# Three of seven second-layer products by a second level of Strassen, in a fused retention and MLP kernel

## The chip, the cores and the metric

The kernel runs on one core of a Trainium2 chip. A core has a matrix engine (TensorE, "PE" in the profile, with its weight loads as "PEld"), a vector engine (VectorE, "DVE"), a scalar engine (ScalarE, "ACT"), GpSimd ("POOL") and a sync engine ("SP") that here issues nearly all transfers; 16 DMA engines carry them. Matrix products are written to PSUM, eight banks of 128 rows by 512 f32; everything else lives in SBUF. The metric is device time in microseconds: 638.29 us, the median of three runs (638.23 to 638.30).

## The reference, cut to what matters

```python
# attention: B=4 heads H=8, S=768 tokens, D=64
state = gamma[None, :, None, None] * state + np.einsum('bhd,bhe->bhde', k[:, :, t], v[:, :, t])
y[:, :, t] = scale * np.einsum('bhd,bhde->bhe', q[:, :, t], state)
# x = y as (B*S, H*D) = (3072, 512); then two layers, 512 -> 2048 -> 512
h = x @ w_in
g = np.maximum(0.01 * h, h)
return (g @ w_out).astype(np.float32)
```

All is float32. The change lies in the last line, the second layer.

## The kernel before, in words

**Tiling.** The sequence is cut into six chunks of 128 tokens (`c` = 0 to 5; with the four batches 512 rows each), the hidden width of 2048 into four units of 512 (`u` = 0 to 3). For each chunk the attention gives `x`, and each unit adds a first layer, a leaky ReLU and a second layer to the chunk's output `o`.

**Strassen (Winograd's form).** Both layers are products of 2 x 2 blocks, made with seven products instead of eight. M1 to M7 take weight blocks (four given, three sums: indices 0 to 6 of a unit) and moving blocks: `g[0..3]`, and the sums `gd[0..2]` that `differences` makes (L609; four subtractions: gd0 = g1 - g0, gd1 = g3 - gd0, gd2 = g2 - gd1, then g1 becomes g3 - g1). In `seven` (matmuls at L662) one product of the second layer is four matmuls of 128 x 128 weights with 256 columns: 28 for a visit. Each float32 matmul shows in the profile as two instructions.

**Chunks 2 to 5, first layer.** There the first layer goes down a second level: each of its seven products is again seven, on blocks of 128. A visit has 49 such matmuls of 128 columns (L1184), in two groups: inner group 0 (four outer products, weights `wa`) and inner group 1 (three, weights `wb`), in the order M1, M5, M4, M6, M2, M3, M7 of `INNER`. ScalarE copies M1's result into M6's bank (L1188) and takes M5, M4, M6 and M2 out of PSUM (L1190 to L1196); VectorE adds M3 and M7 (L606). `outer` then sums these into `g` (two sums after group 0, six after group 1) and ScalarE applies the leaky ReLU (L1226). The weights, sums included, were written to DRAM (`kept`) and are loaded anew for each visit by `load_unit` (L1061 to L1066): 1792 KB for `wa` when inner group 0 has read the old ones, 1344 KB for `wb` after inner group 1.

**The loop around the change.** A visit `n` = 0 to 15 is (chunk 2 + n // 4, unit n % 4). The order is written out by hand: each engine does its work in program order, each instruction when what it needs is there. Visit n does: `differences` of g of n; inner group 0 of visit n+1; the attention of the next chunk in units 0 and 1 (`joint_visit`, L427 and L444, which ends with a load of v and two `decay_v` on GpSimd, L161); then the second layer of n in the order `FUSED`: M1, M5, M6, (scores of the attention to come, L369 and L380, masked by L387), M2, inner group 1 of n+1, M7, `outer` of n+1, M3, M4. In PSUM M1 and M2 share bank A, M6 and M7 B, M5 and M3 C, M4 has D; A to D are banks 5, 4, 7, 6, the inner products use 0 to 3. M1 is copied to B (L755) so that M6 and M7 add onto it, and M7's sum to D (L776) for M4. The output `o` has four blocks of 512 columns; in unit 0 they are set by ScalarE (L746), else VectorE adds (L606), and in unit 3 each is stored (L742). The last visit, 15, has no first layer beside it and uses the order `LAST`: M1, M5, M6, M4, M2, M7, M3.

**Words used below.** "The leaves" are the second-level products of the change; "the tail" is what lies behind visit 14.

Of the kernel before, what the change touches and what calls it, by code (L numbers as in the profile page):

```python
# [9 lines left out]
FP32 = mybir.dt.float32  # L10
# [6 lines left out]
ALU = mybir.AluOpType  # L17

C = 128
# [3 lines left out]
def kernel(  # L23
# [14 lines left out]
    nc = tc.nc  # L38
    NC = S // C
    DM = H * D  # L40
    HP = H // 2
    NU = DF // 512
    N = B * C // 2
# [20 lines left out]
    units = {}  # L64
# [15 lines left out]
    def unit(k):  # L80
        if k not in units:
            units[k] = unit_tile(k, f"w{k}")
        return units[k]

    def block(k, i):

        if k < N_UNITS - 1:
            return unit(k)[:, i]
        return units[k][i // 2][:, i % 2] if i < 6 else last_s4[:, 0]

    gq = dec[:, 0 : HP * C].rearrange("p (j m t) -> p j m t", j=2, t=C)
# [236 lines left out]
    room = {}  # L328
# [169 lines left out]
    def following(c, b):  # L498

        at = (c, b + 2) if b == 0 else (c + 1, 0)  # L500
        return at if at[0] < NC else None
# [5 lines left out]
    TOP = 1151  # L507
    BEND = 2048 + 896 - TOP

    def piece(n):  # L510

        k, h, i = n // 4, n // 2 % 2, n % 2
        if k < N_UNITS - 1:
            return unit(k)[:, 2 * h : 2 * h + 2, i, :]
        new_pair(h)
        return units[k][h][:, :, i, :]
# [88 lines left out]
    def plus(out, a, b):  # L605
        nc.vector.tensor_tensor(out=out, in0=a, in1=b, op=ALU.add)  # L606

    def minus(out, a, b):
        nc.vector.tensor_tensor(out=out, in0=a, in1=b, op=ALU.subtract)  # L609
# [189 lines left out]
        return [x, new_t(c, f"t_{c}")]  # L799

    slot = [0]

    def new_g(c, u):
        i = slot[0]
        slot[0] = 1 - i
        g = work.tile([128, 4, 2, N], FP32, tag=f"g{i}", name=f"g_{c}_{u}")
        gd = work.tile([128, 3, 2, N], FP32, tag=f"gd{i}", name=f"gd_{c}_{u}")
        return u, g, gd

    def run(steps, at):  # L810

# [233 lines left out]
    def sums(c, group):  # L1045
        return lambda: sums_of_x(c, group)

    streamed = []
    N2 = (NC - 2) * NU

    def at_of(n):
        return 2 + n // NU, n % NU
# [15 lines left out]
    def begin_units():  # L1068

        streamed.append(work.tile([128, 7, 4, C], FP32, tag="late4", name="wa"))  # L1070
        load_unit(0, 0)
        flat = work.tile([128, 28 * C], FP32, tag="late6", name="wb")
        streamed.append(flat[:, 0 : 21 * C].rearrange("p (j i n) -> p j i n", j=7, i=3))

    def next_heads():
        for b in range(2):
# [83 lines left out]
    def part_of(moving, s):  # L1160

        block, sums = moving
        if s in (2, 3, 4):
            return sums[:, s - 2]
        k, t = divmod((0, 2, None, None, None, 3, 1)[s], 2)
        return block[:, k, ts(t, C)]

    INNER = (("M1", 0, 0, 0), ("M5", 1, 3, 2), ("M4", 2, 2, 4), ("M6", 3, 4, 3), ("M2", 0, 1, 1),
             ("M3", 1, 5, 5), ("M7", 3, 6, 6))
# [72 lines left out]
    def products(steps, n):  # L1242

        for _ in range(n):
            next(steps, None)
# [35 lines left out]
    for n in range(N2):  # L1281
# [18 lines left out]
            xs[c + 1] = new_x(c + 1)  # L1300
        if visiting:
            joint_visit(c + 1, 2 * u)
        steps = output(c, os[c], [gs.pop(n)], u == 0, u == NU - 1, room=room if more else last_room,
                       order=FUSED if more else LAST, held=held if more else None)
        products(steps, 3)
        if c + 1 < NC and u < 2 and following(c + 1, 2 * u):
            scores_of_pair(*following(c + 1, 2 * u))
        if visiting:
            load_unit(n + 2, 0)
        products(steps, 1)  # L1310
        if c + 1 < NC and u == 1:
            differences(*xs[c + 1])
        if c + 1 < NC and u == 2:
            sums_of_x(c + 1, 0)
        if more:
            inner(n + 1, 1)
            for i in range(2) if visiting else ():
                ahead(c + 2, 2 * u + i)
            products(steps, 1)
            outer(n + 1, 1)  # L1320
        if n + 2 == N2:
            differences(*gs[n + 1][1:])
        products(steps, 3)
# [92 lines left out]
```

## Time and profile before

| what | value |
|---|---|
| median of three runs | 638.29 us |
| the profiled execution | 637.82 us |
| its span, first to last instruction | 636.0 us |
| PE / PEld / DVE / ACT / POOL busy | 99 / 89 / 73 / 42 / 4% |
| chunks 2 to 5 begin at about | 240 us |
| DMA, mean over the span | 178 GB/s |
| HBM read / written | 93.35 / 19.14 MB |
| queue q1 (the transfers that SP issues) | 53.2% of 16 engines |

How to read it: the profile is of one execution, and times in it are microseconds from its first instruction. A group of instructions is told by line, engine, operation, output tile <- input tiles, shape and count; behind the bar stand the busy time in all, the mean nanoseconds of one, and the idle time of the engine just before, with what ended most of it. A timeline line has start, duration and the merged instructions. A matmul's recorded duration overlaps the next one's; the distance of starts is what it costs. For DMAs the number behind the size is the median time from issue to landing. No DMA of the kernel before is issued by GpSimd.

### The profile page before, as it was taken

To read this page: it belongs to the slowest core of one execution; us is meant where nothing else is said; L and a number is where in the kernel's file an instruction comes from. 1 tells how busy PE (TensorE), PEld (TensorE's weight loads), DVE (VectorE), ACT (ScalarE), POOL (GpSimd) and SP (SyncE) were. 2 spreads that over 40 slices of the span, in tenths; PEclk is the share of its full clock that TensorE was granted. 3 is DMA by queue.
4 is the path that set the end of the run, shared out by engine and by line. 5 is a ranking of instruction groups with operands and counts; after the bars stand their busy time and mean duration, and the time that the engine had idled before them with its cause. 6 is when DMAs were issued, how large, how long until landed. Compare 5 with 4: busy or idle time off the path is not lost.

```text
span 636.0 us, 14285 instructions
## 1 busy us (share of the span) xinstructions
PE 628.8 (99%) x6086; PEld 568.8 (89%) x6086; DVE 464.1 (73%) x760; ACT 268.9 (42%) x515; POOL 23.3 (4%) x45
## 2 busy tenths in 40 slices
PE   8999999999999999999999999999999999999997
PEld 5888888888888889899999999999999999999996
DVE  5679769889979986576785666877737768636655
ACT  4876556347343124242352442423433423534421
POOL 2000000000011010101000101000010000000000
PEclk9999999999999999999999999999999999999999
DMA  8941426556863998376735392864455236444201
GB/s 331 404 131 38 128 67 220 148 174 194 283 250 110 351 333 280 103 238 193 259 88 184 120 295 79 268 195 140 137 169 185 87 123 197 154 162 158 87 1 68
DMA packets 87537, 113.42 MB, mean 178 GB/s; under 512 B 3241, under 2 KB 71721, under 8 KB 87473
## 3 DMA queue, kind: packets, MB, share of 16 engines
q1 hardware_dynamic: 87168, 111.88, 53.2%
q8 instruction: 48, 0.79, 0.5%
q10 hardware_dynamic: 304, 0.62, 0.3%
q14 instruction: 17, 0.13, 0.1%
HBM read 93.35 MB, written 19.14 MB: 177 GB/s over the span
## 4 chain that ended last, share of the span: by engine, by line
PE 95%; DVE 2%; ACT 1%; DMA 1%; issue 0%; DVEq 0%; ACTq 0%
PE bank L662 32%; PE bank L1184 27%; PE C_h L662 4%; PE B_o L662 4%; PE A_h L662 4%; PE C_o L662 4%; PE A_o L662 4%; PE B_h L662 4%; PE D_h L662 2%; PE D_o L662 2%; PE d L683 2%; PE bank L369 1%; PE bank L444 1%; PE bank L427 1%; PE bank L380 1%; DMA t<-decay_dram 1%
## 5 line engine op out<-in xcount | busy, mean ns | idle before, releaser
L606 DVE TENSOR_TENSOR made<-made,bank 128x512 f32<-128x512 f32 (+1 forms) x96 | 56.4, 618 | 55.9 <-PE bank L1184 51.5
L606 DVE TENSOR_TENSOR o<-o,bank 128x512 f32<-128x512 f32 (+2 forms) x91 | 58.5, 661 | 51.8 <-PE bank L662 31.2
L662 PE MATMUL bank<-g,w 128*128 128x256 f32 x384 | 89.9, 382 | 0.0
L662 PEld LDWEIGHTS bank<-g,w 128*128 128x128 f32 x384 | 70.7, 190 | 9.2
L1184 PEld LDWEIGHTS bank<-x,wb 128*128 128x128 f32 x672 | 77.6, 192 | 0.8
L1184 PE MATMUL bank<-x,wb 128*128 128x128 f32 x672 | 77.6, 275 | 0.0
L1184 PE MATMUL bank<-x,wa 128*128 128x128 f32 x512 | 67.7, 275 | 0.0
L662 PE MATMUL bank<-gd,w 128*128 128x256 f32 x288 | 66.1, 379 | 0.0
L1184 PEld LDWEIGHTS bank<-x,wa 128*128 128x128 f32 x512 | 63.5, 192 | 1.1 <-ACT made L1194 0.2
L662 PEld LDWEIGHTS bank<-gd,w 128*128 128x128 f32 x288 | 54.7, 190 | 7.4
L1184 PE MATMUL bank<-t,wa 128*128 128x128 f32 x384 | 53.3, 275 | 0.0
L1226 ACT ACTIVATE g<-g 128x512 f32<-128x512 f32 x64 | 39.3, 631 | 30.8 <-DVE g L606 30.8
L1184 PEld LDWEIGHTS bank<-t,wa 128*128 128x128 f32 x384 | 48.0, 192 | 0.0
L1188 ACT COPY bank<-bank 128x512 f32<-128x512 f32 (+1 forms) x32 | 16.7, 520 | 67.8 <-PE bank L1184 67.5
L606 DVE TENSOR_TENSOR g<-made 128x512 f32<-128x512 f32 x64 | 42.7, 688 | 1.2
L755 ACT COPY bank<-bank 128x512 f32<-128x512 f32 x17 | 9.7, 570 | 71.2 <-PE bank L662 71.1
L609 DVE TENSOR_TENSOR gd<-g,gd 128x512 f32<-128x512 f32 x48 | 33.2, 692 | 5.4 <-ACT g L1226 0.5
L776 ACT COPY bank<-bank 128x512 f32<-128x512 f32 x16 | 9.1, 570 | 46.4 <-PE bank L662 46.4
L662 PE MATMUL bank<-g,last 128*128 128x256 f32 x120 | 28.3, 380 | 0.0
L662 PE MATMUL bank<-gd,last 128*128 128x256 f32 (+1 forms) x124 | 27.5, 373 | 0.0
L662 PE MATMUL A_h<-x,w 128*128 128x256 f32 x112 | 26.6, 380 | 0.0
L662 PEld LDWEIGHTS bank<-gd,last 128*128 128x128 f32 x124 | 22.8, 190 | 3.2 <-DVE gd L609 0.3
(223 smaller groups left out, 1030.1 us busy)
## 6 DMA issues: line engine op xcount, KB each, us to landing
wa<-kept SPq DMA_DIRECT2D x16, 1344.0 KB, 7.2
raw<-in_weights_dram SPq DMA_DIRECT2D x31, 512.0 KB, 4.4
wb<-kept SPq DMA_DIRECT2D x16, 896.0 KB, 5.7
wa<-kept SPq DMA_DIRECT2D x16, 448.0 KB, 4.4
wb<-kept SPq DMA_DIRECT2D x16, 448.0 KB, 6.3
out_dram<-o SPq DMA_DIRECT2D x23, 256.0 KB, 3.1
kept<-w SPq DMA_DIRECT2D x12, 448.0 KB, 6.0
qk<-in_qk_dram SPq DMA_DIRECT2D x10, 512.0 KB, 8.0
```

Source lines behind the costliest of these rows:

```text
L369: nc.tensor.matmul(at[j][ts(h, 64), n, m, i], lhsT=x[ts(j, 64), 1, a, ts(h, 64)], rhs=x[ts(j, 64), 0, a, ts(h, 64)], start=(n == 0 and a = ...
L380: nc.tensor.matmul(sums[h][ts(j, 64), n, a], lhsT=key[ts(h, 64), 2 * a + j], rhs=val[ts(h, 64), 2 * a + j], start=(n == 0 and a == 0), sto ...
L427: mm = nc.tensor.matmul(at[n][j][ts(i, 64), m, ts(h, 64)], lhsT=by_half[h][ts(j, 64), n, a], rhs=x[ts(j, 64), 0, a, ts(h, 64)], start=(n = ...
L606: nc.vector.tensor_tensor(out=out, in0=a, in1=b, op=ALU.add)
L609: nc.vector.tensor_tensor(out=out, in0=a, in1=b, op=ALU.subtract)
L662: nc.tensor.matmul(to, lhsT=block(w, sa)[:, k, ts(i, 128)], rhs=rhs[:, k, a:z], start=(first and (i == 0 or split) and n == 0 and k == 0), ...
L683: nc.tensor.matmul(banks[r][:, i, :], lhsT=block(2 * u, r + 2 * kh)[:, k, ts(i, 128)], rhs=x[:, 2 * kh + th, k, :], start=(step == 0 and i ...
L755: nc.scalar.copy(out=bank_of("B"), in_=ps)
L776: nc.scalar.copy(out=bank_of("D"), in_=ps)
L1184: nc.tensor.matmul(ps[q][:, i], lhsT=w[:, j, i], rhs=part_of(moving[i], s), start=(i == 0 and m in ("M1", "M5", "M4")), stop=True, skip_gr ...
L1188: nc.scalar.copy(out=ps[3], in_=ps[0])
L1226: nc.scalar.activation(g[:, i], g[:, i], AF.Prelu, alpha=0.01)
```

## The change

In visits 4 to 14 (chunks 3, 4 and 5, without the very last unit) the second layer no longer runs by `output`. It has two parts:

- `trunk`: M1, M5, M6, M7 as before, 16 matmuls of 256 columns, on banks A, C, B, B. M7's result goes to o2 and o3 in one VectorE addition of 1024 columns (M7 is no longer copied to D); `trunk_taken` adds A to o0, and C to o1 and o3 in one.
- the leaves: M2, M4 and M3 are each cut into seven products of 128-blocks, 21 matmuls of 128 columns. `leaf_sums` makes the moving sums by four subtractions of 384 columns on GpSimd; `load_rows` loads the weights, 1344 KB a visit in three transfers on SP's queue; `leaf_steps` runs the products on banks 6, 7, 2, 5, behind M7, with the leaky ReLUs of the next visit put between its steps; `leaf_results_taken` adds the result to o0..o2, by a DMA of 768 KB issued by GpSimd that accumulates into `o`, or, in unit 3, by three VectorE additions followed by the stores.

In chunk 2 `sums_of_rows` makes the leaves' weight sums on VectorE, and `keep` writes them to DRAM (1344 KB a visit). The blocks 3, 4, 6 of the odd units change places so that those of M2, M3, M4 lie side by side, `g` and `gd` share one tile with `gd` reversed for the same reason, and two pieces of the next chunk's work (`differences(*xs[c + 1])` in unit 1, `sums_of_x` in unit 2) are issued ahead of M1, M5, M6 instead of behind M2. The scratch for DMA descriptors of GpSimd goes from 256 to 512.

```diff
+    PLACE = {3: 4, 6: 3, 4: 6}
     def block(k, i):
         if k < N_UNITS - 1:
-            return unit(k)[:, i]
+            return unit(k)[:, PLACE.get(i, i) if k % 2 else i]
...
     def new_g(c, u):
-        g = work.tile([128, 4, 2, N], FP32, tag=f"g{i}", name=f"g_{c}_{u}")
-        gd = work.tile([128, 3, 2, N], FP32, tag=f"gd{i}", name=f"gd_{c}_{u}")
-        return u, g, gd
+        both = work.tile([128, 7, 2, N], FP32, tag=f"g{i}", name=f"g_{c}_{u}")
+        last_three[c, u] = both[:, 2:5]
+        return u, both[:, 0:4], Reversed(both)
...
+    def sums_of_rows(u):
...
+            plus(r[0], a21, a22)
+            minus(r[1], r[0], a11)
+            minus(r[2], a12, r[1])
+            minus(r[3], a11, a21)
...
+        def keep():
+            for which, blocks in bases:
+                nc.sync.dma_start(out=leaf_kept[u][:, which, 0], in_=blocks[:, :, 0, 0:C])
+                nc.sync.dma_start(
+                    out=leaf_kept[u][:, which, 1:3].rearrange("p i j n -> p i (j n)"),
+                    in_=blocks[:, :, 1])
+            for j, r in enumerate(more):
+                nc.sync.dma_start(out=leaf_kept[u][:, :, 3 + j], in_=r)
...
+    def load_rows(n):
...
+        for to, kept_rows in zip(leaf_weights, (leaf_kept[at_of(n)[1]][:, i] for i in range(3))):
+            nc.sync.dma_start(out=to, in_=kept_rows)
...
+    def by_leaves(n):
+        return n >= NU and n < N2 - 1
+
+    def leaf_sums(n):
...
+        b11, b12, b21, b22 = (three[:, :, k, ts(h, C)] for k in range(2) for h in range(2))
+        for out, a, b in ((made[0], b12, b11), (made[1], b22, made[0]), (made[2], b21, made[1]),
+                          (b12, b22, b12)):
+            nc.gpsimd.tensor_tensor(out=out, in0=a, in1=b, op=ALU.subtract)
+        return [b11, b21, *made, b22, b12]
+
+    def leaf_steps(n, moving):
+        ps = [bank[i][:, 0 : 3 * C].rearrange("p (i n) -> p i n", i=3) for i in (6, 7, 2, 5)]
+        results = leaf_results()
+        for m, q, j, s in INNER:
+            for i in range(3):
+                nc.tensor.matmul(ps[q][:, i], lhsT=leaf_weights[i][:, j], rhs=moving[s][:, i],
+                                 start=(i == 0 and m in ("M1", "M5", "M4")), stop=True,
+                                 skip_group_check=True)
+            if m == "M1":
+                nc.scalar.copy(out=ps[3], in_=ps[0])
+            elif m == "M3":
+                plus(results[:, :, 1], results[:, :, 1], ps[1])
+            elif m == "M7":
+                plus(results[:, :, 3], results[:, :, 3], ps[3])
+                plus(results[:, :, 2], results[:, :, 2], ps[3])
+            else:
+                nc.scalar.copy(out=results[:, :, {"M5": 3, "M4": 2, "M6": 1, "M2": 0}[m]],
+                               in_=ps[q])
+            yield
...
+    def leaf_results_taken(c, o, final):
+        results = leaf_results()
+        if not final:
+            nc.gpsimd.dma_start(out=o[:, 0:3].rearrange("p i k n -> p (i k n)"),
+                                in_=results.rearrange("p i q n -> p (i q n)"), accum_op=ALU.add)
+            return
+        for i in range(3):
+            plus(o[:, i], o[:, i], results[:, i].rearrange("p (k h) n -> p k (h n)", k=2))
+            nc.sync.dma_start(out=out[c, i], in_=o[:, i])
...
+    def trunk_taken(o, first):
+        if first:
+            nc.scalar.copy(out=o[:, 0], in_=room["A"])
+            nc.scalar.copy(out=o[:, 3], in_=room["C"])
+            plus(o[:, 1], o[:, 1], room["C"])
+        else:
+            plus(o[:, 0], o[:, 0], room["A"])
+            plus(o[:, 1:4:2], o[:, 1:4:2],
+                 room["C"].unsqueeze(1).to_broadcast([128, 2, 2, N]))
...
         if visiting:
             joint_visit(c + 1, 2 * u)
+            if by_leaves(n):
+                load_rows(n)
...
+        moving = leaf_sums(n) if by_leaves(n) else None
...
+        if by_leaves(n):
+            steps = trunk(c, os[c], part, u == 0, u == NU - 1)
...
+        if by_leaves(n):
+            if scores_next and u > 0:
+                products(steps, 2)
+            trunk_taken(os[c], u == 0)
+            if scores_next and u == 0:
+                products(steps, 2)
+        else:
+            products(steps, 1)
+        if c == 2:
+            keep = sums_of_rows(u)
         if more:
             inner(n + 1, 1)
...
+            if c == 2:
+                keep()
             products(steps, 1)
-            outer(n + 1, 1)
+            later = [] if by_leaves(n) else None
+            outer(n + 1, 1, later)
+        if by_leaves(n):
+            products(steps, 1)
+            leaves = leaf_steps(n, moving)
+            for count, ready in ((4, 3), (1, 1)) if scores_next else ((1, 1), (3, 2), (1, 1)):
+                products(leaves, count)
+                for _ in range(ready):
+                    later.pop(0)()
+            products(leaves, 8)
+            leaf_results_taken(c, os[c], u == NU - 1)
+        if more and by_leaves(n + 1) and not (at_of(n + 1)[0] + 1 < NC and at_of(n + 1)[1] < 2):
+            load_rows(n + 1)
```

## The prediction

> **What bounds the kernel now.** I read the page's busy shares and its chain first, then windows over chunks 2 to 5, then the timeline of one visit. The page:
>
> ```profile
> PE 628.8 (99%) x6086; PEld 568.8 (89%) x6086; DVE 464.1 (73%) x760; ACT 268.9 (42%) x515; POOL 23.3 (4%) x45
> ...
> PE 95%; DVE 2%; ACT 1%; DMA 1%; issue 0%; DVEq 0%; ACTq 0%
> ```
>
> TensorE is the bound and 95% of the chain. Windows over the changed stages (length, busy PE, PEld, DVE, ACT, POOL, clock, DMA share, GB/s):
>
> ```profile
> 345.00:455.00 110.00, 110.00 (x1155) 102.42 (x1154) 77.27 (x131) 42.50 (x80) 4.48 (x8) 1.00 0.57 182
> 455.00:560.00 105.00, 105.00 (x1014) 98.13 (x1013) 72.90 (x123) 39.26 (x72) 2.43 (x6) 1.00 0.47 147
> 560.00:619.00 59.00, 59.00 (x390) 55.13 (x389) 31.94 (x52) 23.08 (x43) 0.00 (x0) 1.00 0.32 101
> ```
>
> TensorE has no gap here at clock 1.00: time falls only if it is issued less work, and rises by each stall. VectorE is at 70%, DMA at about half. A busy PE overstates one matmul (ends are modelled), so I price by pitch, start to start, in visit 6's timeline:
>
> ```profile
> 405.88 0.38 PE L1184 MATMUL bank<-x,wa 128*128 128x128 f32 x2
> ...
> 412.13 1.89 PE L662 MATMUL bank<-g,w 128*128 128x256 f32 x8
> ...
> 419.04 4.85 PE L1184 MATMUL bank<-x,wb 128*128 128x128 f32 x42
> ...
> 423.73 1.46 PE L662 MATMUL bank<-g,w 128*128 128x256 f32 x6
> ```
>
> One f32 matmul is two instructions. From 412.13 to 419.04 stand four products of 8: 6.91/32 = 0.2159 us each, 1.727 us a product. From 419.04 to 423.73 stand three second-level products: 4.69/42 = 0.1117 us. Inner group 0 takes 412.13 - 405.88 = 6.25 us.
>
> **TensorE's share of the change.** A product by seven leaves costs 14 x 0.1117 = 1.563 us, 0.164 less. Three products in each of visits 4 to 14 are 33: **-5.40 us**. The pattern (three matmuls to a weight, one bank, 128 columns) is that of inner group 1, so I take its pitch. Nothing else leaves TensorE; 632.9 is the floor.
>
> **One visit after**, from t = 0 at the end of inner group 1: M7 to 1.73, leaves to 6.42, next inner group 0 to 12.67, M1, M5, M6 to 17.85, inner group 1 to 22.54 (visits with attention are longer, with M7 ahead of t = 0). Durations:
>
> ```profile
> L606 DVE TENSOR_TENSOR o<-o,bank 128x512 f32<-128x512 f32 x81 | 54.5, 685 | 50.9 <-PE bank L662 31.2 <-ACT bank L776 19.7
> L1226 ACT ACTIVATE g<-g 128x512 f32<-128x512 f32 x64 | 39.3, 631 | 30.8 <-DVE g L606 30.8
> ...
> L606 DVE TENSOR_TENSOR made<-made,bank 128x384 f32<-128x384 f32 x48 | 25.2, 552 | 44.8 <-PE bank L1184 44.0
> ...
> L1190 ACT COPY made<-bank 128x384 f32<-128x384 f32 x16 | 7.7, 478 | 3.3 <-PE bank L1184 3.3
> ```
>
> In a run of VectorE operations the 512-wide start 0.61 us apart (617.76, 618.37, 618.97 in the last visit), so queues are counted with 0.61.
>
> *VectorE.* Out go six sums of o, 6 x 0.685 = 4.11. In come 0.685 twice and two 1024-wide ones, not in the trace: 685 + 4 x (685 - 552) = 1.22 each, 3.81 together; three leaf sums 3 x 0.552 = 1.66; in visits 7 and 11 three final sums, 2.06. So +1.4 a visit, +3.4 in those two. The queue runs: inner sums to 1.3, six outer sums to 5.0, M7's to 6.1, leaf M3 to 6.7, leaf M7 to 7.6 (its matmuls end at 6.42), differences to 10.1. M5 wants the first difference at 14.4, 6 us after it is made: hidden. If VectorE fell 6 us behind, all of it would count.
>
> *ScalarE.* It interleaves five leaf copies with four leakies. M1's copy is done by 3.1, the first leaky by 3.7, M5, M4, M6 by 5.1; leaf M7 wants M6's bank free at 5.75. Slack 0.65 us; past it each us of lateness in each visit is TensorE's. I take 0. In visit 12 (first, no attention) three 512-wide copies (o1, o0, o3) now stand between M6 and inner group 1's first copy, 0.51 apart: that copy ends 2.2 us after M6, and inner M6 wants it at 3 x 0.67 = 2.0: **+0.3**.
>
> *GpSimd* gets four 384-wide subtractions a visit. Its row is decay's 512-wide 1.04 us, so 0.8 each, 3.2 together. They start after the third difference (9.5) and are wanted at 24.3. In visits 4, 5 and 8 they queue behind the decays, which wait for a v load (4.5 us); 3.6 us of slack stays.
>
> ```profile
> 203.93 2.60 POOL L161 TENSOR_TENSOR v<-v,dec 128x512 f32<-128x512 f32 x2 [1.56 <-DMA v<-in_kv_dram]
> 204.22 1.42 DVE L609 TENSOR_TENSOR last<-last,last 128x512 f32<-128x512 f32 x1
> ...
> 363.06 2.04 POOL L161 TENSOR_TENSOR v<-v,dec 128x512 f32<-128x512 f32 x2 [4.54 <-DMA v<-in_kv_dram]
> ```
>
> Side by side, a VectorE operation on two SBUF inputs goes from 0.69 to 1.42 and GpSimd's pair from 2.04 to 2.60. The Trainium skill (SBUF — State Buffer, "Who interferes with whom") speaks against the change: with two SBUF inputs VectorE's second comes over the interface that GpSimd reads by, and in its rule of thumb the later one blocks fully. By the rule VectorE waits out up to 3.2 us a visit; by the row it loses half of the overlap, some 1.6, worst in visits 7 and 11, where sums for the next chunk lie there. Either fits in the 6 us: 0 taken.
>
> *The accumulating DMA*, 768 KB, issued by POOL at about 7.7. The trace has none. Near rows (KB each, us to landing):
>
> ```profile
> wa<-kept SPq DMA_DIRECT2D x16, 1344.0 KB, 7.2
> ...
> wb<-kept SPq DMA_DIRECT2D x16, 896.0 KB, 5.7
> wa<-kept SPq DMA_DIRECT2D x16, 448.0 KB, 4.4
> ...
> out_dram<-o SPq DMA_DIRECT2D x23, 256.0 KB, 3.1
> ```
>
> A plain one is between 448 and 896: 5.3 us. Reading the target too at worst doubles the bytes: 1536 KB, about 8 us. The skill (DMA: Bandwidth & Descriptors, "Anatomy of one DMA — SWDGE (gpsimd) path") gives 2.0 us plus bytes over 436 GB/s: estimated 3.8 us, less than our rows show for plain copies, so I use the rows: x = 7, ends 5.3 and 8, with an open top as nothing here bounds descriptor writing. It must land before M6's sum into o1, at 18; behind that wait VectorE holds A's and C's sums and inner group 1's. TensorE notices when M7 wants bank B at 22.5: x up to 14. The tail is tighter, for there is no inner work after visit 14:
>
> ```profile
> 619.81 1.89 PE L662 MATMUL bank<-g,last 128*128 128x256 f32 x8
> 620.90 0.68 DVE L609 TENSOR_TENSOR gd<-g 128x512 f32<-128x512 f32 x1
> ...
> 621.64 5.48 PE L662 MATMUL bank<-gd,last 128*128 128x256 f32 x28
> ```
>
> Visit 15's M1 begins at 6.42, M5 at 8.15, M7 at 15.3, and M7 needs bank B, whose sum into o1 (0.7) waits for the DMA: x up to 6.9 is free. x = 7 gives **+0.1** (the ends: 0, +1.1). M5 waits 0.1 us for its difference now (ready 621.58); after, it is ready at 8.3 against 8.15: **+0.1** more.
>
> *Loads.* load_rows adds 1344 KB a visit on SP's queue (three issues), behind the leaves or, with attention, behind the v load and ahead of k and the next wa. A plain visit then moves 3136 KB of units, 1344 and at worst 1536, some 6.2 MB, where 22.5 us at 182/0.57 = 319 GB/s carry 7.2. wa (7.2 us) has 16.3 us from issue to use: hidden even at twice its time; beyond, its lateness is paid in each visit.
>
> *Chunk 2.* sums_of_rows puts four 384-wide sums (2.2 us; the last visit 2.6) ahead of inner group 1's M3, which comes 4.0 us in, and 1344 KB of stores on SP behind wb and qk; the next loads in that queue are some 10 us off. The differences of x (2.8) and group 0's sums move ahead of M6's sum, into VectorE's wait for M6. Hidden; 0.
>
> *Other moves.* In visits 4, 5 and 8 M7 goes ahead of inner group 1 as cover for the masks of the scores, 1.73 us as M2 was before; it needs bank B, whose M6 was taken some 2 us of scores earlier. In visits 7 and 11 the stores of o0 to o2 leave some 3 to 4 us later in SP's queue, at 9.4; the next write of o is M6's copy at 20 or later and a store lands in 3.1: hidden. Dropping M7's copy to D takes 0.57 us from a ScalarE that waits there for TensorE: 0. The new places of blocks and of g, and the larger scratch, add no instruction: 0.
>
> **Sum.** -5.40 + 0.3 + 0.1 + 0.1 = -4.9. On the profiled execution: span 636.0 to 631.1, its time 637.82 to 632.9. The median of the runs, 638.29, is 0.47 above that execution: **633.4**.
>
> **Rivals.** *A, the accumulating DMA is slow* (ends slower). Each us of x over 6.9 is paid once in the tail; at x = 11.8 the gain is gone. Above 14, six visits without attention (6, 7, 10, 11, 13, 14, fed by the visit before) pay as well: x = 16 gives 633.3 + 9.1 + 6 x 2 = 654. Slower by 0.2% from about x = 13. For it: no row for accumulation, and POOL's descriptor writing is unmeasured. Against: 8 us by doubled bytes. *B, VectorE or ScalarE come late to the leaves*: half a us over the 0.65 slack in eleven visits gives 639, with 0.2 us 635.6. For it: the skill's blocking, and VectorE near 20 of 22.5 us in visits 7 and 11. Against: its order leaves 6 us. *C, loads land late* by 0.5 us in eleven visits: 638.9. Against: the 16 us.
>
> **Chances.** A measurement of this kernel tells 0.2% (1.3 us) from no change: faster is below 637.0, slower above 639.6. Forecast, 632.4 to 635: 0.68. B or C in small measure, or A with x of 8 to 10, 635 to 637: 0.13. The same in larger measure: 0.07 within 0.2%. A beyond 13, or B and C full: 0.12 slower. Faster 0.81. Range 632.4 to 639: the floor less 0.5, up to where A or B have just eaten the gain; it leaves out some 0.14.
>
> **What would show it.** Right: leaves in 4.69 us for 42 instructions; PE without gaps in visits 4 to 14 but 0.3 us in visit 12; VectorE's wait for DMA at M6's sum none but in visit 15. Wrong: TensorE waiting on ACT copies within the leaves (B), on VectorE behind a DMA wait (A), on wa (C); a leaf pitch over 0.1117.

## The result and the profile after

The changed kernel takes **633.83 us** (median of four runs, 633.29 to 633.91); the kernel before took 638.29 us beside it (638.23 to 638.34). The ratio is 0.9928 with a 95% interval of 0.9911 to 0.9945: 4.5 us faster. The profiled execution took 633.81 us with a span of 632.1, 3.9 us less than the 636.0 of before.

The two differences, 4.5 and 3.9, are not the same because the median of before lay 0.47 above its profiled execution and that of after only 0.02. Four later groups of runs had the kernel before at 637.96, 637.84, 637.66 and 637.88, so 638.29 was on the high side. Where a few tenths count, I go by spans and by the starts of the same work in two traces.

First the busy shares and the chain on the page of the kernel after:

```profile
PE 624.7 (99%) x6284; PEld 570.5 (90%) x6284; DVE 498.1 (79%) x803; ACT 283.5 (45%) x559; POOL 81.4 (13%) x98
...
PE 90%; DMA 5%; ACT 2%; DVE 2%; issue 0%; SPq 0%; DVEq 0%; ACTq 0%
```

TensorE is still the bound: 99% busy, with 4.1 us less of it, although it issues 198 instructions more (half as wide). Everything around it is fuller: VectorE by 34 us, GpSimd by 58, ScalarE by 15. The 5% of DMA in the chain lie ahead of the changed visits: the first 24 us, and 8.4 us of a load that begins at 241.30. The same three windows as before (length, busy PE, PEld, DVE, ACT, POOL, clock, DMA share, GB/s):

```profile
345.00:455.00 110.00, 110.00 (x1246) 105.00 (x1245) 88.98 (x142) 49.40 (x99) 25.31 (x27) 1.00 0.86 269
455.00:560.00 105.00, 104.30 (x1085) 99.31 (x1084) 83.86 (x131) 43.94 (x87) 27.95 (x29) 1.00 0.77 236
560.00:619.00 59.00, 58.92 (x448) 56.23 (x447) 40.92 (x64) 28.94 (x59) 11.18 (x11) 1.00 0.60 168
```

VectorE goes from 70 to 81% in the first, DMA from 0.57 to 0.86, and TensorE keeps clock 1.00. The one gap worth looking for is in the second window: PE 104.30 of 105. The waits of PE and of its weight loads name it (total, times, longest):

```profile
PEld bank L1299 <- DVE x L468: 1.1, 1, 1.1
...
PEld bank L668 <- DVE g L615: 0.4, 1, 0.4
...
PEld bank L1348 <- ACT bank L1352: 0.3, 1, 0.3
```

In this kernel L1299 is a matmul of `trunk`, L1261 one of the leaves, L1348 of the first layer, L668 of `seven`, L468 the scaling of the next chunk's tokens, L1352 the copy of inner M1, L612 and L615 `plus` and `minus`, L1252 a subtraction of `leaf_sums`, L1283 the accumulating DMA.

The work itself came out at the forecast price. In the timeline of the leaves of visit 6 (two matmuls to an f32 product, so 42 instructions) the first starts at 422.94 and the next inner group 0 at 427.62:

```profile
422.94 0.61 PE L1261 MATMUL bank<-g,w 128*128 128x128 f32 x4
...
427.22 1.62 DVE L612 TENSOR_TENSOR w<-w,bank 128x384 f32<-128x384 f32 x3 [0.34 <-PE bank L1261]
...
427.62 0.39 PE L1348 MATMUL bank<-x,wa 128*128 128x128 f32 x2
```

That is 4.68 us against the 4.69 of inner group 1, with no gap: VectorE waits for TensorE here (the bracket), not the reverse.

**Where the 3.9 us come from.** I took the start of inner group 1 of each visit in both traces. Between visits without attention it recurs every 22.54 us where it was 23.03: 0.49 less, three products at 0.164, as forecast. Beside that stand these differences:

| place | against before, us |
|---|---|
| 33 products, 0.164 each | -5.40 |
| before chunk 3 (0.20 of it already in the first 34 us, which the change doesn't touch) | +0.29 |
| visit 12, inner group 1: 559.40 to 564.43 = 5.03, where it was 563.88 to 568.57 = 4.69 | +0.34 |
| visit 5, from the inner group 1 of visit 4 to its own: 27.06, where it was 27.66 and three products less would be 27.17 (before stood still for 0.2 ahead of M1, after for 0.1 ahead of M7) | -0.1 |
| visit 9, from the start of M1 to inner group 1: 6.25, where the same three products took 5.28 | +0.97 |
| from inner group 1 of visit 14 to the end: 27.28, where it was 26.06 and should be 26.06 + 1.73 - 0.49 = 27.30 (M2 now lies behind that start) | 0.0 |
| sum | -3.9 |

The one large piece that the forecast doesn't have is visit 9. Here is the timeline of before and then of after:

```profile
487.25 0.69 DVE L606 TENSOR_TENSOR made<-made 128x512 f32<-128x512 f32 x1
487.78 1.59 PEld L662 LDWEIGHTS bank<-g,w 128*128 128x128 f32 x8
...
487.98 0.69 DVE L606 TENSOR_TENSOR g<-made 128x512 f32<-128x512 f32 x1
488.59 1.41 DVE L466 TENSOR_TENSOR x<-bank,dec 128x256 f32<-128x256 f32 x4
...
489.61 1.24 PE L662 MATMUL bank<-gd,w 128*128 128x256 f32 x5
```

```profile
484.89 0.99 POOL L1252 TENSOR_TENSOR w<-g 128x384 f32<-128x384 f32 x1
485.00 1.43 DVE L612 TENSOR_TENSOR made<-made 128x512 f32<-128x512 f32 x1
485.53 1.59 PEld L1299 LDWEIGHTS bank<-g,w 128*128 128x128 f32 x8
...
485.96 1.33 POOL L1252 TENSOR_TENSOR w<-g,w 128x384 f32<-128x384 f32 x1
486.53 1.30 DVE L612 TENSOR_TENSOR g<-made 128x512 f32<-128x512 f32 x1
...
487.76 1.40 DVE L468 TENSOR_TENSOR x<-bank,dec 128x256 f32<-128x256 f32 x4
488.22 2.89 PEld L1299 LDWEIGHTS bank<-g,w 128*128 128x128 f32 x14 [1.10 <-DVE x L468]
```

M1's weight loads start at 487.78 before and 485.53 after; counted from there, VectorE's scaling of x starts 0.81 us in before and 2.23 us in after. The first of its four instructions frees bank 7, into which M5 writes. Before, that one ended at about 489.0 and M5 began at 489.61, without a wait: 0.6 us of room. Now x is 1.42 us later against M1, and M5 waits. What is ahead of it on VectorE is the same two sums as before, but each takes 1.3 to 1.4 us instead of 0.69, and beside them, new, run GpSimd's subtractions.

### The profile page after: what moved, and what is told of

Its sections match the earlier page's. It is cut to its first block, busy times and chain, and to the rows that moved or that the text cites. A ratio compares the mean times of both kernels' runs of the same rounds, so it can differ in the third digit from the quotient of the medians.

```text
span 632.1 us, 15063 instructions
## 1 busy us (share of the span) xinstructions
PE 624.7 (99%) x6284; PEld 570.5 (90%) x6284; DVE 498.1 (79%) x803; ACT 283.5 (45%) x559; POOL 81.4 (13%) x98
## 4 chain that ended last, share of the span: by engine, by line
PE 90%; DMA 5%; ACT 2%; DVE 2%; issue 0%; SPq 0%; DVEq 0%; ACTq 0%
PE bank L1348 26%; PE bank L1299 12%; PE bank L668 11%; PE bank L1261 8%; PE C_h L668 4%; PE B_o L668 4%; PE A_h L668 4%; PE A_o L668 4%; PE C_o L668 4%; PE B_h L668 4%; PE D_o L668 2%; PE D_h L668 2%; DMA x_words<-in_weights_dram 1%; DMA wa<-kept 1%; DMA in<-in_kv_dram 1%; PE bank L371 1%
## 5 line engine op out<-in xcount | busy, mean ns | idle before, releaser
L612 DVE TENSOR_TENSOR made<-made,bank 128x512 f32<-128x512 f32 (+1 forms) x96 | 56.1, 617 | 39.9 <-PE bank L1348 35.9
L1348 PEld LDWEIGHTS bank<-x,wb 128*128 128x128 f32 x672 | 77.6, 192 | 1.1 <-ACT bank L1352 0.3
L1348 PE MATMUL bank<-x,wb 128*128 128x128 f32 x672 | 77.9, 275 | 0.1
L612 DVE TENSOR_TENSOR o<-o,bank 128x512 f32<-128x512 f32 (+3 forms) x75 | 55.2, 767 | 24.3 <-ACT bank L782 6.2
L615 DVE TENSOR_TENSOR g<-g 128x512 f32<-128x512 f32 x96 | 64.1, 688 | 5.3 <-ACT g L1390 0.6
L1348 PE MATMUL bank<-x,wa 128*128 128x128 f32 x512 | 67.6, 275 | 0.0
L1299 PE MATMUL bank<-g,w 128*128 128x256 f32 x288 | 66.1, 382 | 0.7 <-DVE x L468 0.7
L1348 PEld LDWEIGHTS bank<-x,wa 128*128 128x128 f32 x512 | 62.8, 192 | 0.3
L1299 PEld LDWEIGHTS bank<-g,w 128*128 128x128 f32 x288 | 53.2, 190 | 8.0 <-DVE x L468 1.1
L1348 PE MATMUL bank<-t,wa 128*128 128x128 f32 x384 | 53.4, 275 | 0.1
L1348 PEld LDWEIGHTS bank<-t,wa 128*128 128x128 f32 x384 | 48.0, 192 | 0.3 <-DMA wa<-kept 0.3
L612 DVE TENSOR_TENSOR g<-made 128x512 f32<-128x512 f32 x64 | 44.0, 709 | 3.0
L1352 ACT COPY bank<-bank 128x512 f32<-128x512 f32 (+1 forms) x32 | 16.6, 520 | 60.1 <-PE bank L1348 59.8
L668 PE MATMUL bank<-g,w 128*128 128x256 f32 x168 | 38.0, 382 | 0.0
L668 PEld LDWEIGHTS bank<-g,w 128*128 128x128 f32 x168 | 31.3, 190 | 4.2
L668 PE MATMUL bank<-g,last 128*128 128x256 f32 (+1 forms) x148 | 32.6, 375 | 0.0
L668 PEld LDWEIGHTS bank<-g,last 128*128 128x128 f32 x148 | 27.0, 190 | 3.9 <-DVE g L615 0.4
L1261 PE MATMUL bank<-g,w 128*128 128x128 f32 x176 | 26.8, 275 | 0.0
L668 PE MATMUL A_h<-x,w 128*128 128x256 f32 x112 | 26.6, 380 | 0.0
L1303 ACT COPY bank<-bank 128x512 f32<-128x512 f32 x11 | 6.3, 570 | 41.1 <-PE bank L1299 41.1
L1283 POOL DMA_DIRECT2D o<-w x9 | 8.1, 903 | 125.2 <-DVE g L615 65.6
```

The costliest lines, as they stand in the source:

```text
L668: nc.tensor.matmul(to, lhsT=block(w, sa)[:, k, ts(i, 128)], rhs=rhs[:, k, a:z], start=(first and (i == 0 or split) and n == 0 and k == 0), ...
L1261: nc.tensor.matmul(ps[q][:, i], lhsT=leaf_weights[i][:, j], rhs=moving[s][:, i], start=(i == 0 and m in ("M1", "M5", "M4")), stop=True, sk ...
L1283: nc.gpsimd.dma_start(out=o[:, 0:3].rearrange("p i k n -> p (i k n)"), in_=results.rearrange("p i q n -> p (i q n)"), accum_op=ALU.add)
L1299: nc.tensor.matmul(ps[x][:, i, :], lhsT=block(2 * u + 1, sa)[:, k, ts(i, 128)], rhs=rhs[:, k, :], start=(start and i == 0 and k == 0), sto ...
L1303: nc.scalar.copy(out=ps["B"], in_=ps["A"])
L1348: nc.tensor.matmul(ps[q][:, i], lhsT=w[:, j, i], rhs=part_of(moving[i], s), start=(i == 0 and m in ("M1", "M5", "M4")), stop=True, skip_gr ...
```

## The experiments

**The theories.** P: in visit 9 GpSimd reads SBUF while VectorE makes those two sums; that stretches them, x comes late and bank 7 with it. Q, its rival: VectorE simply has too much to do. The expectations use these letters. In the diffs, "-" is the changed kernel. Where an edit adds lines, the line numbers of its profile are up to 4 higher (in experiment 1, L613 and L616 are `plus` and `minus`; in 1, 9 and 10, L1303 a matmul of `trunk`, L1352 one of the first layer, L1253 or L1252 GpSimd's work in `leaf_sums`, L1285 the DMA). The stage ahead of the change, where these kernels don't differ from the changed one, ends 0.3 to 0.4 us earlier in experiments 1, 2, 4 and 5 than in it (the first inner group 1 starts at 242.47 to 242.56 instead of 242.84), and their times came out 0.3 us or so under what was expected. What an edit gains is therefore read inside its trace.

**1. GpSimd waits for x in visit 9.** The same work, but the first subtraction of that visit doesn't start until VectorE has scaled x.

```diff
-            nc.gpsimd.tensor_tensor(out=out, in0=a, in1=b, op=ALU.subtract)
+            made_now = nc.gpsimd.tensor_tensor(out=out, in0=a, in1=b, op=ALU.subtract)
+            if n == 9 and out is made[0]:
+                tc.add_manual_dep(made_now.ins, tokens[0].name, IN_ORDER,
+                                  reason="tokens first")
```

> In visit 9 the first of the four GpSimd subtractions waits until VectorE has made the x of the joint visit; nothing else changes. Theory P (shared port): visit 9 loses 0.9 us because these subtractions run beside two VectorE sums on two SBUF inputs and double them (1.43 and 1.30 for 0.69 us), which makes the x late and holds M5. Then the wait of TensorE on x goes, 632.9 us (0.9 less than 633.83), and the stretching moves to the differences of x, behind which nobody waits. Rival Q (VectorE's longer queue, whoever runs beside it): no change, 633.8.

Measured: 632.53 us (632.4 to 632.56), ratio to before 0.9913 (0.9899 to 0.9926), span 630.8. The timeline:

```profile
484.68 0.69 DVE L613 TENSOR_TENSOR made<-made 128x512 f32<-128x512 f32 x1
485.21 5.45 PE L1303 MATMUL bank<-g,w 128*128 128x256 f32 x24
485.47 0.69 DVE L613 TENSOR_TENSOR g<-made 128x512 f32<-128x512 f32 x1
486.08 1.41 DVE L468 TENSOR_TENSOR x<-bank,dec 128x256 f32<-128x256 f32 x4
...
488.25 2.78 DVE L616 TENSOR_TENSOR t<-x,t 128x512 f32<-128x512 f32 x2
```

The sums are at 0.69 again, M1, M5 and M6 run as one piece of 24 instructions, and the contention has moved onto the differences of x (2.78 us for two, where two take 1.42), for which no one waits: TensorE has no gap from M1 on. From M1 to inner group 1 it takes 5.28 us again (485.21 to 490.49), 0.97 less. P says this and Q doesn't: no work was removed from VectorE.

**2. GpSimd writes instead of reading.** In visit 9 the four subtractions become memsets: the same instructions in the same places, writing the same tiles, but reading nothing. The Trainium skill (SBUF — State Buffer, "Who interferes with whom") says that a VectorE instruction with two SBUF inputs is held up by a GpSimd instruction that reads SBUF, and not by one that only writes it.

```diff
-            nc.gpsimd.tensor_tensor(out=out, in0=a, in1=b, op=ALU.subtract)
+            if n == 9:
+                nc.gpsimd.memset(out, 0.0)
+            else:
+                nc.gpsimd.tensor_tensor(out=out, in0=a, in1=b, op=ALU.subtract)
```

> In visit 9 alone GpSimd fills the four blocks with zeros instead of subtracting: it writes SBUF at the same place of the program and reads nothing (visit 9's leaves are then not the reference's). If it is GpSimd's reading that stretches VectorE's sums (theory P as the Trainium skill words it): the two sums of visit 9 take 0.69 again, TensorE's wait on x goes, 0.9 us less than the changed kernel. If any GpSimd work on SBUF beside VectorE does it: the sums that overlap a fill stay near 1.3 to 1.4 us and some of the wait stays.

Measured: 632.61 us (632.47 to 632.8), ratio 0.9918 (0.9904 to 0.9931), span 631.0.

```profile
484.70 0.77 POOL L1253 MEMSET w<- 128x384 f32 x2
484.84 0.69 DVE L612 TENSOR_TENSOR made<-made 128x512 f32<-128x512 f32 x1
485.41 0.42 POOL L1253 MEMSET x<- 128x384 f32 x1
485.64 0.69 DVE L612 TENSOR_TENSOR g<-made 128x512 f32<-128x512 f32 x1
```

GpSimd is at work right beside both sums (a memset takes some 0.4 us), and they take 0.69 us. So it is the reads that stretch them, as the page says. Its rule for such a pair ("Summary: rules for kernel authors"), that the second one to issue is blocked until the first is done, fits the lines of the changed kernel too. The first sum starts at 485.00 and ends at 486.43, that is 0.55 behind the end of the subtraction that was under way (485.88). The second subtraction, started at 485.96, ends at 487.29, 0.86 behind the end of that sum; the second sum ends at 487.83, 0.54 behind that subtraction. Each of these is about 0.14 us less than the instruction takes alone (0.69 and 1.00). The two engines alternate, and each sum pays for one subtraction: 0.74 and 0.61 us.

**3. The sums on VectorE.** If Q is wrong and VectorE has room, the four subtractions can go there, away from the contention.

```diff
-            nc.gpsimd.tensor_tensor(out=out, in0=a, in1=b, op=ALU.subtract)
+            nc.vector.tensor_tensor(out=out, in0=a, in1=b, op=ALU.subtract)
```

> The four subtractions of the leaves run on VectorE in all eleven visits, in the same place of the program, 4 x 0.55 = 2.2 us a visit more for it; GpSimd has none. Theory P: no stretched pairs, visit 9's stall goes (the subtractions are queued behind x), and 2.2 us fit into VectorE's slack: 632.9 to 633.2. Rival Q: VectorE is what is scarce, 2.2 us more in each visit show up as new waits of TensorE: 634.5 or more.

Measured: 635.36 us (634.95 to 636.91), ratio 0.9964 (0.995 to 0.9978), span 633.1: slower than the changed kernel. P's number (632.9 to 633.2) missed, and Q's (634.5 or more) was met. The wait in visit 9 was gone, as P said, but in visit 5 there was a new one:

```profile
391.93 1.39 DVE L1252 TENSOR_TENSOR w<-g 128x384 f32<-128x384 f32 x1
...
394.43 0.55 DVE L1252 TENSOR_TENSOR g<-g 128x384 f32<-128x384 f32 x1
394.89 0.68 DVE L612 TENSOR_TENSOR o<-o,bank 128x512 f32<-128x512 f32 x1
...
395.63 1.99 PE L1299 MATMUL bank<-g,w 128*128 128x256 f32 x8 [1.99 <-DVE o L612]
```

In visits 4, 5 and 8 M7 stands ahead of inner group 1 and wants bank B 2.1 us after M6 (the time of the scores' matmuls, 391.54 to 393.6). In visit 5 the sum that empties B stands on VectorE behind 3.0 us of subtractions. In visits 4 and 8, of unit 0, ScalarE empties it, and they take no longer than in the changed kernel (27.47 and 28.72 us from one inner group 1 to the next, in both). 632.1 - 1.0 + 2.0 = 633.1 is the span measured. So neither theory holds in its simple form: VectorE isn't short of time over a visit, but a queue in order has single places with little room.

**4. ScalarE's copies in visit 12.** There o0, o1 and o3 are copied behind M6, ahead of inner M1's copy. Here two are issued between M5 and M6.

```diff
-        products(steps, 3)
+        early = by_leaves(n) and u == 0 and not scores_next
+        products(steps, 2 if early else 3)
+        if early:
+            nc.scalar.copy(out=os[c][:, 0], in_=room["A"])
+            nc.scalar.copy(out=os[c][:, 3], in_=room["C"])
+            products(steps, 1)
+            plus(os[c][:, 1], os[c][:, 1], room["C"])
...
-            trunk_taken(os[c], u == 0)
+            if not early:
+                trunk_taken(os[c], u == 0)
```

> In visit 12 the copies of A to o0 and of C to o3 are issued ahead of M6's copy instead of behind it. If ScalarE's three copies in a row cost visit 12 its 0.34 us (inner group 1's first copy late), 633.5, and the gap of inner group 1 in visit 12 goes from 5.03 back to 4.69 us. If something else holds it, 633.8.

Measured: 633.24 us (633.14 to 633.57), ratio 0.9925 (0.9912 to 0.9937), span 631.5. The changed kernel first, then this one:

```profile
559.40 5.19 PE L1348 MATMUL bank<-x,wb 128*128 128x128 f32 x42
559.65 0.58 ACT L1306 COPY o<-bank 128x512 f32<-128x512 f32 x1 [2.93 <-PE bank L1299]
...
560.60 0.60 ACT L1325 COPY o<-bank 128x512 f32<-128x512 f32 x1
561.08 0.51 ACT L1352 COPY bank<-bank 128x384 f32<-128x384 f32 x1
```

```profile
559.43 0.59 ACT L1306 COPY o<-bank 128x512 f32<-128x512 f32 x1 [1.20 <-PE bank L1299]
560.04 0.46 ACT L1352 COPY bank<-bank 128x384 f32<-128x384 f32 x1
```

The copy of inner M1 (L1352) starts 0.87 us behind the start of inner group 1 instead of 1.68, and the group takes 4.69 us (559.17 to 563.86) instead of 5.03. The 0.34 is this queue.

**5. Both mends together.**

```diff
+    (the edits of 1 and of 4)
```

> Both edits together (GpSimd's wait in visit 9, the order of copies in visit 12). The stalls lie in different visits, so their savings add: 633.83 - 0.9 - 0.34 = 632.6. If one only moved the other's loss, 632.9 or more.

Measured: **632.26 us** (632.06 to 632.62), ratio 0.9911 (0.9896 to 0.9926), span 630.4. It is the fastest version here, 1.6 us under the changed kernel and 5.7 under the kernel before beside it (637.96). The floor is reached: the span is 5.6 below before, which is the 5.40 of TensorE's work, the 0.1 of visit 5 and 0.16 by which the stage ahead of the change ended earlier.

**6. All that lies around, without the leaves.** `by_leaves` is false throughout: chunk 2 still makes and stores the weight sums, the moves and new places stay, and chunks 3 to 5 use seven whole products.

```diff
-        return n >= NU and n < N2 - 1
+        return False
```

> Everything of the change stays but no visit uses the leaves: chunk 2 still makes and stores the weight sums, blocks and g keep their new places, the early differences stay; visits 4 to 15 run the old second layer. Unit 3's weight sums overwrite blocks that the old path then reads, so the values of chunks 3 to 5 differ. If the side work is hidden, as the prediction has it: 638.3 (within 0.3 of before). If chunk 2's sums, stores and new orders cost something: above 638.6, with gaps of TensorE in visits 0 to 3.

Measured: 637.77 us (637.35 to 639.91) beside 637.84 before; ratio 1.0 (0.9994 to 1.0007), span 636.1. The work in chunk 2 costs nothing that can be measured, although VectorE has 9 us more of it there (240 to 345: 82.37 busy here, 73.38 before).

**7. Leaves in chunks 4 and 5 alone.** Chunk 3 is done with seven whole products; seven visits have the leaves.

```diff
-        return n >= NU and n < N2 - 1
+        return n >= 2 * NU and n < N2 - 1
```

> The leaves in seven visits (8 to 14) instead of eleven; chunk 3 runs the old second layer (its values differ, as unit 3's weight sums overwrite blocks it reads). If each visit saves 0.49 us of TensorE's work and the stalls are those of visits 9 and 12: 633.83 + 4 x 0.49 = 635.8. If the gain is a fixed one (early orders, fewer copies) and not by the visit: 633.8.

Measured: 636.94 us (636.06 to 638.68), ratio 0.9984 (0.9977 to 0.9991), span 635.4; it gained 0.9 (0.6 in the span) where about 2 was expected. Inside, each visit without attention lost its 0.49 again (22.54 for 23.03), and visit 12 paid its 0.34. Visit 9 lost more than in the changed kernel, 1.8 us (24.81 from one inner group 1 to the next, where 23.03 is the work, as in experiment 1), and the tail lost 0.5. With 0.16 ahead of the change, 7 x 0.49 - 1.8 - 0.3 - 0.5 - 0.2 = 0.6 accounts for the span.

The 1.8 us are not the wait of the changed kernel. VectorE's sums are stretched there too (1.43 and 1.30 us from 486.96 and 488.49), but TensorE stops within M1, ahead of the last of its four matmuls, which starts at 490.66 instead of 488.9, with nothing that the profile shows to wait for ("issue"). M5 follows at 491.09 and finds x ready since 490.12. What TensorE waited for stays open, and so this run says nothing for or against P.

In the tail the accumulating DMA landed 6.40 us after its issue (620.56 to 626.95), and TensorE's M7 then waited for bank B: 0.3 us of the 0.5.

**8. VectorE adds instead of the accumulating DMA.**

```diff
-        if not final:
-            nc.gpsimd.dma_start(out=o[:, 0:3].rearrange("p i k n -> p (i k n)"),
-                                in_=results.rearrange("p i q n -> p (i q n)"), accum_op=ALU.add)
-            return
         for i in range(3):
             plus(o[:, i], o[:, i], results[:, i].rearrange("p (k h) n -> p k (h n)", k=2))
-            nc.sync.dma_start(out=out[c, i], in_=o[:, i])
+            if final:
+                nc.sync.dma_start(out=out[c, i], in_=o[:, i])
```

> The leaves' result is added to o by three VectorE additions in all visits; no accumulating DMA. 2.06 us more of VectorE in nine visits. If VectorE's six us of slack are there, interior visits lose nothing but visit 9 (x later by up to 0.5) and visit 15, where the additions stand ahead of the differences that M5 waits for (+1.8): 635.5 to 636.2. If the accumulating DMA cost time inside, this is faster than 633.8. If VectorE has no slack, 2 us in each of nine visits: over 640.

Measured: 636.31 us (635.57 to 638.98), 0.1 over the expected range, ratio 0.9981 (0.9972 to 0.9989), span 634.2, 2.1 more than the changed kernel. From the first inner group 1 to the last it takes 0.45 us more (362.43 and 361.98); most of the loss, 1.9, is in the tail, first in the changed kernel, then here:

```profile
617.06 2.88 DVE L615 TENSOR_TENSOR g<-g 128x512 f32<-128x512 f32 x4
617.79 0.88 POOL L1283 DMA_DIRECT2D o<-w  x1 [16.42 <-DVE g L615]
617.80 8.53 PEld L668 LDWEIGHTS bank<-g,last 128*128 128x128 f32 x44 [0.39 <-DVE g L615]
...
623.69 2.04 DVE L612 TENSOR_TENSOR o<-o,bank 128x512 f32<-128x512 f32 x3 [3.03 <-DMA o<-w]
```

```profile
617.39 1.90 DVE L612 TENSOR_TENSOR o<-o,w 128x512 f32<-128x512 f32 x3
619.20 2.81 DVE L615 TENSOR_TENSOR g<-g 128x512 f32<-128x512 f32 x4
619.94 8.53 PEld L668 LDWEIGHTS bank<-g,last 128*128 128x128 f32 x44 [2.39 <-DVE g L615]
```

The three additions stand ahead of the differences that M5 waits for: 2.39 us of wait instead of 0.39. So the DMA is worth 2 us, once, in visit 15, and little in the other visits. The same lines give its length with little else in flight: issued at 617.79, waited out at 623.69, **x about 6 us**. VectorE waits 3.03 us for it and TensorE does not.

**9. Six smaller accumulating DMAs.** The 768 KB go in six pieces of 128 KB, in the order in which their sums are wanted.

```diff
-            nc.gpsimd.dma_start(out=o[:, 0:3].rearrange("p i k n -> p (i k n)"),
-                                in_=results.rearrange("p i q n -> p (i q n)"), accum_op=ALU.add)
+            for i in (0, 2, 1):
+                for k in range(2):
+                    nc.gpsimd.dma_start(
+                        out=o[:, i, k],
+                        in_=results[:, i, 2 * k : 2 * k + 2].rearrange("p q n -> p (q n)"),
+                        accum_op=ALU.add)
```

> The accumulating DMA is cut into six of 128 KB, those of o1 last, so it ends some 4.5 us later (five more issues of 0.9 us on GpSimd). By the deadlines of the prediction (6.9 us after the request in the tail, 14 inside): the tail's 6.0 becomes 10.5, +3.6; inside, 9.2 becomes 13.7, nothing, save up to 0.4 each in visits 5 and 9, where GpSimd's marker for the joint visit stands behind the issues: 637.4 to 638. If the DMA has more slack than I worked out, 633.8; if the inside deadline is nearer than 14, over 645.

Measured: 770.06 us (767.93 to 772.32), ratio 1.207 (1.2041 to 1.2099), 132 us away from what was expected. One visit of it:

```profile
421.07 0.88 POOL L1285 DMA_DIRECT2D o<-w  x1 [10.30 <-ACT w L1272]
...
435.76 0.87 POOL L1285 DMA_DIRECT2D o<-w  x1 [6.64 <-issue]
439.68 0.87 POOL L1285 DMA_DIRECT2D o<-w  x1 [3.05 <-issue]
...
447.03 0.87 POOL L1285 DMA_DIRECT2D o<-w  x1 [2.12 <-issue]
...
449.82 2.42 DVE L612 TENSOR_TENSOR o<-o,bank 128x512 f32<-128x512 f32 x3 [17.30 <-DMA o<-w]
...
450.56 3.78 PE L1303 MATMUL bank<-g,w 128*128 128x256 f32 x8 [14.27 <-DVE o L612]
```

GpSimd issues one piece in 0.88 us and then stands still, 3 us or more from one to the next, 7 beside loads, with nothing that the profile shows to wait for ("issue"). A piece lands in 2.7 us (up to 7.2), and each of the 45 that follow another of their visit is issued 0.26 to 0.32 us after that one has landed: one is in flight at a time. This is rival A in full: x is 449.82 - 421.07 = 28.7 us and TensorE waits 14.3, so inside chunks 3 to 5 the deadline is at 14.4, where the forecast had 14. The waits come to 75.3 us in the six visits that the prediction names (`PE bank L1303 <- DVE o L612`), 10.3 in the tail and 31.1 in visits 5 and 9, where a GpSimd memset that the attention waits for stands behind the pieces: 116.7. Much of the other 20 us of span is the clock. Windows ahead of, in and behind that gap (columns as above):

```profile
421.00:433.00 12.00, 12.00 (x87) 11.39 (x86) 9.25 (x18) 4.07 (x9) 1.77 (x2) 1.00 1.08 365
433.00:450.50 17.50, 3.29 (x30) 3.10 (x28) 0.68 (x2) 1.90 (x4) 5.91 (x7) 0.69 0.56 127
450.50:456.00 5.50, 5.44 (x17) 4.73 (x18) 5.36 (x10) 0.34 (x1) 1.53 (x2) 0.50 0.00 0
```

The clock falls during the rest of 14 us (0.69 on average in that row), TensorE is granted 0.50 when it starts again, and its product from 450.56 takes 3.6 us instead of 1.73.

**10. The same six with a larger descriptor scratch.** If the scratch is what lets only one in at a time, doubling it lets in more.

```diff
-                   dynamic_dma_scratch_size=512)
+                   dynamic_dma_scratch_size=1024)
```

> The six accumulating DMAs of 128 KB as before, with GpSimd's descriptor scratch at 1024 instead of 512. With 512 each of the six starts as the one before has landed (3.0 us apart, 7 and more among loads), and the last lands 28.7 us after the first request. If the scratch holds one at a time and 1024 holds two, they overlap in pairs and the last lands after some 15 to 19 us: 650 to 690 us. If six accumulations into one tile are in series for another reason: 770 as with 512.

Measured: 652.09 us (651.88 to 655.18), ratio 1.0234 (1.0215 to 1.0254), within the range of the first theory.

```profile
410.43 2.69 POOL L1285 DMA_DIRECT2D o<-w  x3 [11.16 <-ACT w L1272]
417.52 0.85 POOL L1285 DMA_DIRECT2D o<-w  x1 [4.40 <-issue]
```

Three now go back to back before GpSimd stands still, and the fourth to sixth of every visit start 0.25 to 0.40 us after the piece three places ahead has landed. So the scratch sets how many are in flight; why twice the size takes three and not two stays open, and larger ones weren't tried.

**11. Without the leaves' weight loads.** From visit 5 on the leaves use the weights that are there (the output is not the reference's); 1344 KB a visit are gone from SP's queue. It ran beside the changed kernel itself.

```diff
-        for to, kept_rows in zip(leaf_weights, (leaf_kept[at_of(n)[1]][:, i] for i in range(3))):
+        for to, kept_rows in () if n > NU else zip(leaf_weights, (leaf_kept[at_of(n)[1]][:, i] for i in range(3))):
```

> The leaves' weights are loaded once, in visit 4, and kept: ten of the eleven loads of 1344 KB are left out, so visits 5 to 14 use unit 0's weights and the values differ. If the loads are hidden, as the prediction has it: the time of the changed kernel within 0.3 us, while the accumulating DMA (9.2 us among the loads, 6.0 alone in the tail) comes down inside too. If they delay the other loads or the accumulation by enough to matter: faster by 0.5 us or more.

> The changed kernel unchanged, beside the next two on one chip, for their comparison: 0.9928 of before, 633.2 to 633.8.

Measured: 633.29 us (633.19 to 633.61) without the loads, 634.02 (633.67 to 635.27, 0.2 over what was expected) for the changed kernel; spans 631.6 and 632.1. Taken by itself the difference of the medians, 0.7, is what was expected if the loads matter. But the half microsecond of the spans isn't theirs: the first inner group 1 starts at 242.52 and 242.90, ahead of the first load that is left out, and from there to the last it is 361.92 us in both. The other 0.14 lie in the last 6 us of the kernel, where none of these loads is left. The loads cost nothing on the path. What they do is slow the accumulating DMA, which takes 9.2 us in the middle in the changed kernel and 6.6 without them.

## Why the prediction was right, and where it wasn't

**Direction and cause: right.** The time falls by what TensorE issues less, 5.40 us, at the forecast pitch (4.68 us for the leaves), in all visits. Without the leaves nothing is left of it (experiment 6); with both mends it comes out in full (experiment 5).

**Visit 12, +0.3: right**, 0.34, at the place and for the reason given (experiment 4); the copy ends 2.2 us behind M6 (561.59 against 559.40), as worked out.

**The tail, +0.1 and +0.1: nothing of it was lost, in part by luck.** The accumulating DMA took 5.8 us where 7 was taken. But the 6.9 that were called free are not there: in experiment 7 it took 6.4 and TensorE waited for it. GpSimd issues it 1.87 us after the leaves (615.92 to 617.79), where the prediction had 1.28, and so about 6.2 us are free. Two errors cancelled; with x = 7 the loss would have been some 0.9 us, by estimate from these lines. M5's loads wait 0.39 us for their difference, where they waited 0.34 before. The deadline in the tail also shows in experiment 9 (10.3 us of wait there), and that inside too (14.4 from the first piece, against 14).

**Inside, x = 7: too low.** It is 9.2 in the middle, 7.3 to 10.4 inside, beyond the upper end of 8, because of the loads in flight at the same time (6.6 without them). It cost nothing, as the deadline of 14 was not reached: VectorE waited once, 3.09 us in visit 14, where the prediction had no such wait, and TensorE never. The prediction's other figure, 3.8 us, is under even the 5.8 of the tail.

**Loads, chunk 2, the moves: 0, right** (experiments 11 and 6).

**GpSimd beside VectorE, 0: wrong, 1.0 us.** The step that failed is "Either fits in the 6 us". The time that VectorE loses was forecast well: 1.6 us a visit by the row, 3.2 by the rule if VectorE stands behind all four subtractions. In visit 9 the two sums lose 1.35 us and the first difference of x another 0.31 (1.00 us at 489.19, where one takes 0.69): 1.7. The rule is right for one pair of instructions (experiment 2), but the scaling of x, which reads PSUM, runs beside the third subtraction at its usual 1.40 us, and so not every subtraction is paid. A subtraction alone takes 1.00 us, not the 0.8 that was scaled from the row of 512. The room is what was wrong. The 6 us were worked out for one reader, M5's wait for its difference. VectorE's queue has other readers: in visit 9 bank 7, which the attention hands to M5 through the scaling of x, and there the room was 0.6 us. In visit 5 it is bank B (experiment 3). Visit 9 is the only one of the attention's visits that pays because the subtractions start there at once; in visits 4, 5 and 8 GpSimd first does the decays, as the forecast says, but chunk 5 is the last and has none behind it in visit 9. The forecast listed where the decays delay the subtractions, and not where their absence brings them forward, into VectorE's sums.

**The median: right in part by luck.** On the profiled execution the forecast was 632.9 and 633.81 came out. Visit 9 is 1.0 of that; the 0.3 that were lost before chunk 3 and the 0.3 that visit 5 and the tail didn't take cancel. The 0.47 that was added for the median of before hid half of it: the median of after stood 0.02 above its profiled execution.

## What to carry to other kernels

A slack holds for one reader: for each engine whose queue grows, list every bank and every tile that something behind the new work hands on, visit by visit, and take the least. When work moves to an engine with time to spare, ask also where that engine has nothing to do ahead of it: there the new work starts early, and what it reads collides with work that was undisturbed. A bulk transfer off the path may be slow up to its deadline, which can be computed; check that it stays one transfer, since several small ones queued behind each other cost about thirty times the gain here.

## What the hardware showed that was not expected

- GpSimd subtractions, which read SBUF, doubled a VectorE sum of two SBUF inputs (0.69 to 1.30 and 1.43 us), GpSimd memsets, which only write it, left it alone (0.69), and in a collision the engines took turns, so GpSimd is stretched too (1.00 to 1.33).
- Accumulating DMAs of 128 KB issued by GpSimd went one at a time with a descriptor scratch of 512 and three at a time with 1024: 770 us and 652 us for the same six pieces a visit.
- An accumulating DMA of 768 KB within SBUF took 5.8 us nearly alone, 6.6 with the leaves' weight loads left out and 9.2 with them; issuing it took GpSimd 0.9 us.
- After 14 us without matmuls TensorE was granted half its clock for the next 5.5 us (0.50 from 450.50 to 456.00 in experiment 9).
- The stage ahead of the change ends up to 0.4 us apart in different kernels that don't differ there (242.5 to 242.9), so differences of this size between spans say nothing about the change.
